# First chunk of a spectral mixer moved from tile to tile, its other chunks read in long runs, and GpSimd given more of the weight splitting

## The chip, the cores and the metric

The kernel runs on one core of one Trainium2 chip. The metric is the device time of one execution in microseconds: the median over the runs of the kernel before and after the change.

## The reference

One transformer-like block over x of 4096 rows and 640 columns, in float32: an adaptive layer norm, a Fourier mixer over the rows (AFNO), and a gated feed-forward part.

```python
mod = (silu(c) @ w_mod).reshape(1, 6, 1, 640)
sa, ca, ga, sb, cb, gb = (mod[:, i] for i in range(6))
h = layernorm(x) * (1 + ca) + sa
# AFNO: FFT over rows and columns axes (rfft2 with H = 1), 4 blocks of 160 channels,
# two complex layers w1, w2 with bias, ReLU between, soft threshold 0.01, inverse FFT
x = x + ga * irfft2(shrink(layer2(relu(layer1(rfft2(h))))))
h = layernorm(x) * (1 + cb) + sb
x = x + gb * ((silu(h @ w_gate) * (h @ w_up)) @ w_down)
```

## The kernel before

The Fourier transform of 4096 rows is made in two steps, 4096 = 128 x 32: row n is n1 * 32 + n2. **Stage A** works on 8 tiles `xa[t]` of 128 partitions (n1) and four values of n2, each a slice of 640 columns. For each tile DVE and GpSimd make the layer norm's statistics (`ln_stats`), ACT and DVE normalise (`ln_apply`), PE multiplies by the cosine and sine table `fa` (`dft_a`, line 407: four matmuls of 512 columns, one for each slice, and a fifth for the remaining 128 of all four) and ACT or DVE write the result back over the tile (`evac_a`, lines 414 to 418). The order of the columns of `fa` decides which frequency lands on which partition.

**Chunks.** The 128 partitions of a result hold eight chunks of 16 rows. **Stage B** wants one chunk at a time, with the 32 values of n2 on partitions, so the rows are turned through DRAM: `write_s1(t, f)` (line 338) writes the rows of tile t that belong to family f into the scratch tensor `s1[f]` (family 0: chunks 0 and 1, family 1: 2 and 3, family 2: 4 to 7), and `load_g(ch)` (line 307) reads a chunk back with four transfers into a tile `g` of 128 partitions and four slices of 640. Two such tiles exist (`gx`). A chunk can be read when all eight tiles of its family are written. Chunk 0 is read in two pieces: the rows of tiles 0 to 6 on GpSimd's queue, those of tile 7 on SyncE's queue.

**The loop.** Then a software pipeline of 32 steps p = 4 * ch + b runs over chunks and channel blocks: `stage_b` (line 542) finishes the transform into a PSUM bank, `evac_b` and `evac_r` (lines 549, 550, 572, 582) split it into a high and a low part for the rounded fp32r matmuls, `stage_l1` (603, 616) and `stage_l2` (649) are the two complex layers, `move_x` (665) turns the result `tt` by moves between tiles, `shrink` is the threshold, and `stage_i` the first half of the inverse transform, which writes to the scratch tensor `s2`. In the loop `mod_load` (478) brings pieces of `w_mod` into the buffer `wm`, and `mod_add` sums them on DVE. The feed-forward part comes after it.

**Weights.** `w1` and `w2` are split into high and low parts as well: `prep_weights` lists jobs for the tiles a, b and c (c holds the remainders), `weights_high` (280 on ACT, 278 on GpSimd) and `weights_low` (283 on DVE) do them. `w1` goes through ACT and DVE after stage A, the high parts of `w2` through GpSimd.

**Order.** All of this is one written order (`manual_schedule`): every engine and every queue executes its instructions in the order in which the code emits them, and SyncE's queue carries nearly all transfers. `moves(t)` emits what that queue does after tile t. The tiles `xa` and the pool `p2` (which holds `acc`, `cl`, `wx`, `bx`, `w2a` to `w2c`, `wm`, `tt`, `xx` and others) share the same memory, so an instruction that writes a `p2` tile waits until the rows of the `xa` tile beneath it are written out. PSUM has the tags b0 and b1 with one bank each and p1, p2, p3 with two each.

Of the kernel before, what the change touches and what calls it, by code (L numbers as in the profile page):

```python
# [9 lines left out]
OP = mybir.AluOpType  # L10
# [36 lines left out]
def constants():  # L47
# [9 lines left out]
    for ch in range(8):  # L57
        for p in range(2):
            for ri in range(2):
                for jj in range(4):  # L60
                    r = 4 * (2 * p + ri) + jj
                    m = 4 * (16 * (ch % 2) + r) + (0, 2, 1, 3)[ch // 2]
                    k = 2 * (4 * ORDER[ch] + jj) + p
                    th = tau * ((n1 * k) % 128) / 128
                    fa[:, m] = np.cos(th) if ri == 0 else -np.sin(th) if k else (-1.0) ** n1
# [106 lines left out]
def body(tc, x, w1, b1, w2, b2, wg, wu, wd, c, wm, k_fa, k_tb, k_tx, k_bm, k_bx, k_ga, k_ge, k_id, out, dbg=None):  # L172
# [8 lines left out]
    ov = out.rearrange("a b (n1 n2) d -> (a b n1) n2 d", n2=N2)  # L181
    s1 = [nc.dram_tensor(f"s1{f}", (n, N2, D), F32, kind="Internal").ap() for f, n in enumerate((32, 32, 64))]
    s2 = nc.dram_tensor("s2", (128, N2, D), F32, kind="Internal").ap()
# [16 lines left out]
    with ExitStack() as top:  # L200
# [33 lines left out]
        with ExitStack() as af:  # L234
# [49 lines left out]


            af.enter_context(tc.manual_schedule())
            nc.sync.dma_start(fa, k_fa)
# [10 lines left out]

            def load_g(ch, lo=0, hi=32, dma=None):
                if ch < 4:  # L300
                    src = s1[ch // 2].rearrange("(c q j) n d -> c q n j d", c=2, q=4)[ch % 2]
                else:
                    src = s1[2].rearrange("(c q j f) n d -> f c q n j d", c=2, q=4, f=2)[ch // 2 - 2, ch % 2]
                if lo == 0:
                    gs[ch] = fx.tile([P, 4, D], F32, tag="gx", bufs=2, name=f"g{ch}")
                for q in range(4):
                    (dma or nc.sync).dma_start(gs[ch][4 * lo + q:4 * hi:4], src[q, lo:hi])

# [15 lines left out]
            with tc.tile_pool(name="sp", bufs=1) as sp:  # L324
# [10 lines left out]


                def write_s1(t, f):
                    nc.sync.dma_start(s1[f][:, 4 * t:4 * t + 4, :], xas[t][(0, 2, 1)[f]:128:(4, 4, 2)[f]])

# [7 lines left out]

                def moves(t):
                    write_s1(t, 0)
                    if t == 0:  # L350
                        load_x(6)
                        nc.sync.dma_start(c5, c)
                    elif t == 1:
                        load_x(7)
                        raws[1] = load_weights(sp, w1, "1")
                    elif t == 2:
                        nc.sync.dma_start(wm1, wm[:, 1])
                    elif t == 3:
                        load_tb(0)
                        nc.sync.dma_start(b1m, b1[:, 0:8].rearrange("p (r b) -> p r b", r=2))  # L360
                        nc.sync.dma_start(b1r, b1[0:64, 8:12])
                        raws[2] = load_weights(rp, w2, "2")
                    elif t < 7:
                        if t == 6:
                            load_g(0, 0, 28, pool)
                        for f in (1, 2):
                            write_s1(t - 3, f)
                    else:
                        load_g(0, 28, 32)

# [29 lines left out]
                def dft_a(t):  # L400

                    xnr = xas[t].rearrange("p a (b e) -> p a b e", b=NB)
                    for i in range(5):
                        j = 5 * t + i
                        pa = (bank0(j // 4, [P, 512], f"pa{t}_{i}") if j % 4 == 0
# [4 lines left out]
                def evac_a(t):  # L410
                    xa = xas[t]
                    for i in range(5):
                        if t == 7 and i % 2:
# [9 lines left out]
                for t in range(8):  # L423
# [8 lines left out]
                    if t == 2:  # L432
                        act.activation(sc, c5, AF.Silu)
                    moves(t)

# [3 lines left out]
                for job in prep_weights(raws[1], w1a, w1b, w1c, True):  # L439
                    weights_high(*job)  # L440
                    weights_low(*job)

            hp = af.enter_context(tc.tile_pool(name="hp", bufs=1, reuse_waits="tile"))
            load_g(1)
            load_tb(1)
            b2t = hp.tile([P, 2, NB, BS], F32, name="b2t")
            nc.sync.dma_start(b2t, b2.rearrange("r b o -> (r b o)").partition_broadcast(P))
            for t in (0, 4, 5, 6, 7):
                write_s1(t, 1)
            load_g(2)  # L450
            load_tb(2)
            for t in (0, 4, 5, 6, 7):
                write_s1(t, 2)
            stx.close()

            nc.sync.dma_start(idn, k_id)
            nc.sync.dma_start(tx, k_tx)
            pool.dma_start(bm.rearrange("p a b c -> p (a b c)"), k_bm)
            p2 = af.enter_context(tc.tile_pool(name="p2", bufs=1, side="right", reuse_waits="tile"))

            acc = p2.tile([P, D], F32, name="acc")
            cl = p2.tile([P, D], F32, name="cl")
            wx = p2.tile([P, P], F32, name="wx")
            bx = p2.tile([P, 2, 128], F32, name="bx")
            w2a = p2.tile([P, NB, 640], F32R, name="w2a")
            w2b = p2.tile([P, NB, 640], F32R, name="w2b")
            w2c = p2.tile([P, NB, 640], F32R, name="w2c")
            prep2 = prep_weights(raws[2], w2a, w2b, w2c, False)
            for job in prep2:
# [6 lines left out]
            def mod_load(m, k):  # L476
                wmts[m, k] = p2.tile([P, D], F32, tag="wm", bufs=1, name=f"wm{m}_{k}")
                nc.sync.dma_start(wmts[m, k], wm[:, m, k, :])
# [57 lines left out]

            def stage_b(ch, t):
                g, tb = gs[ch], tbs[ch]
                pb = bank0(1 if t == 4 else 0, [P, 2, 256], f"pb{ch}_{t}")
                col = slice(128 * t, 128 * t + 128)  # L540
# [186 lines left out]


            for b in range(3):
                stage_b(0, b)  # L730
                if b == 0:
                    stage_b(0, 4)
                evac_b(0, b)
                evac_r(0, b)
# [33 lines left out]
            for p in range(LAST + 1):  # L768
# [28 lines left out]
                if p == 0:  # L797
                    for job in prep2[3:]:
                        weights_low(*job)
                if b == 3 and 2 < ch + 2 < NCH:  # L800
                    load_g(ch + 2)
# [9 lines left out]

            def load_first():
                x2 = fx.tile([P, 4, D], F32, tag="gx", bufs=2, name="x2_0")
                nc.sync.dma_start(x2, xv[:, 0:4, :])
                x2s[0] = x2
# [5 lines left out]
            for p in range(LAST + 1, NP):  # L821
# [4 lines left out]
                if p == LAST + 1:  # L826
                    on(shrink, p - 5)
                elif p == LAST + 2:
                    load_first()
                on(shrink_high, p - 5)  # L830
                on(stage_l2, p - 1)
                on(stage_i, p - 6)
                on(shrink_low, p - 5)
            on(shrink, LAST - 1)
            on(shrink_high, LAST - 1)
# [48 lines left out]
            def first_norm(i):  # L884
                mv, rs, nm = fst[i]
                xn = p2.tile([P, D], F32, tag="co" if i < 2 else "wm", bufs=2 if i < 2 else 1, name=f"xn0_{i}")
                act.activation(xn, x2[:, i, :], AF.Identity, bias=nm, scale=rs)
# [347 lines left out]
```

## Time and profile before

| | |
|---|---|
| runs of the kernel before | 1502.13, 1502.27, 1503.7 us; median 1502.27 us |
| profiled execution | 1502.37 us, its span 1500.6 us |
| PE busy | 1456.5 us, 97% of the span |
| DVE, ACT, POOL busy | 871.8, 587.7, 117.0 us |
| mean granted TensorE clock | 0.993 |

The span runs from the first instruction to the last; the profiled execution's time holds 1.8 us more. PE is TensorE's matmul row, DVE VectorE, ACT ScalarE, POOL GpSimd, SP SyncE; a "q" behind an engine's name means its queue of instructions that issue transfers. In the chain of waits a row gives the start, the length and what the end of the execution was waiting for then.

### The profile page before, as it was taken

The numbers are of one execution on the slowest core, as the hardware profiler recorded it, in microseconds if no ns is written. First come the engines' busy times: TensorE is split into PE (matmuls) and PEld (weight loads), VectorE is DVE, ScalarE is ACT, GpSimd is POOL, SyncE is SP. The second block draws the span as 40 slices with busy tenths as digits, with TensorE's granted clock in tenths as the row PEclk, the third lists the DMA queues.
The fourth block names the chain that finished last, engine by engine and source line by source line (L and its number), as shares of the span: only waits on it lengthen the run. The fifth ranks groups of instructions, "written<-read, shape, count | busy, mean of one in ns | idle before, by whom it ended". The sixth has DMA issues, their size and how long they took to land.

```text
span 1500.6 us, 20793 instructions
## 1 busy us (share of the span) xinstructions
PE 1456.5 (97%) x8114; PEld 1292.2 (86%) x8114; DVE 871.8 (58%) x1598; ACT 587.7 (39%) x1034; POOL 117.0 (8%) x215
## 2 busy tenths in 40 slices
PE   7599999989999999999999999999999999999998
PEld 2399999868989898989898989898889988898888
DVE  8478888877475437543844374447444744564433
ACT  7569989746232314231323132313231322223220
POOL 5400100030010001000100010001000100000000
PEclk9799999999999999999999999999999999999999
DMA  9946556647432423241324132513241324223210
GB/s 377 319 168 188 167 160 184 206 135 233 140 88 84 111 74 97 85 138 47 100 84 138 53 102 75 154 36 102 80 140 53 94 80 131 62 71 89 70 44 35
DMA packets 183057, 179.92 MB, mean 120 GB/s; under 512 B 19312, under 2 KB 153648, under 8 KB 180016
## 3 DMA queue, kind: packets, MB, share of 16 engines
q1 hardware_dynamic: 173728, 152.56, 34.0%
q0 software_dynamic: 3904, 14.91, 3.0%
q10 hardware_dynamic: 5328, 11.14, 2.0%
q8 instruction: 63, 1.03, 0.3%
q14 instruction: 34, 0.28, 0.1%
HBM read 137.95 MB, written 31.46 MB: 113 GB/s over the span
## 4 chain that ended last, share of the span: by engine, by line
PE 84%; DVE 5%; ACT 4%; DMA 4%; POOL 1%; SPq 1%; issue 1%; DVEq 0%; ACTq 0%; POOLq 0%
PE pd L1143 26%; PE pg L1050 8%; PE pg L1049 8%; PE pg L1051 8%; PE pu L1050 8%; PE pu L1049 8%; PE pu L1051 8%; PE pc L649 1%; PE pl L603 1%; PE pa L407 1%; DMA xx<-tt 1%; PE pb L542 1%; PE pt L1031 1%; DMA s<-xa 1%; DMA g<-s 1%
## 5 line engine op out<-in xcount | busy, mean ns | idle before, releaser
L1143 PE MATMUL pd<-wdh,ah 128*128 128x320 f32 x1664 | 384.4, 310 | 0.1
L1143 PEld LDWEIGHTS pd<-wdh,ah 128*128 128x128 f32 x1664 | 282.4, 188 | 1.0 <-DVE yo L1147 0.4
L1143 PE MATMUL pd<-wdl,ah 128*128 128x320 f32 x832 | 257.0, 309 | 0.0
L1044 DVE TENSOR_TENSOR wl<-wr,wh 128x640 fp32r<-128x640 f32 x216 | 177.5, 822 | 121.5 <-ACT wh L1043 121.5
L1050 PE MATMUL pg<-ht,wh 128*128 128x512 f32 x555 | 216.2, 389 | 0.0
L1049 PE MATMUL pg<-ht,wh 128*128 128x512 f32 x555 | 216.1, 389 | 0.0
L1051 PE MATMUL pg<-ht,wl 128*128 128x512 f32 x555 | 216.0, 389 | 0.0
L1049 PE MATMUL pu<-ht,wh 128*128 128x512 f32 x515 | 200.8, 390 | 0.0
L1050 PE MATMUL pu<-ht,wh 128*128 128x512 f32 x515 | 200.6, 390 | 0.0
L1051 PE MATMUL pu<-ht,wl 128*128 128x512 f32 x515 | 200.4, 389 | 0.0
L1107 ACT ACTIVATE sg<-pg 128x512 f32<-128x512 f32 x104 | 62.2, 598 | 336.2 <-PE pg L1051 335.3
L1120 ACT ACTIVATE ah<-sg 128x512 fp32r<-128x512 f32 x104 | 65.8, 632 | 295.4 <-DVE sg L1119 295.4
L1043 ACT ACTIVATE wh<-wr 128x640 fp32r<-128x640 f32 x216 | 157.1, 728 | 41.5 <-DVE x L1148 38.2
L1147 DVE TENSOR_TENSOR yo<-pd,gbb 128x320 f32<-128x320 f32 x128 | 62.7, 490 | 183.7 <-PE pd L1143 183.7
L1143 PEld LDWEIGHTS pd<-wdl,ah 128*128 128x128 f32 x832 | 156.3, 188 | 0.6
L1051 PEld LDWEIGHTS pg<-ht,wl 128*128 128x128 f32 x555 | 104.2, 188 | 21.8
L1119 DVE TENSOR_TENSOR sg<-pu,sg 128x512 f32<-128x512 f32 x104 | 71.7, 689 | 88.1 <-PE pu L1051 88.1
L1049 PEld LDWEIGHTS pg<-ht,wh 128*128 128x128 f32 x555 | 104.2, 188 | 21.0
L1050 PEld LDWEIGHTS pg<-ht,wh 128*128 128x128 f32 x555 | 104.2, 188 | 21.0
L1121 DVE TENSOR_TENSOR ah<-sg,ah 128x512 fp32r<-128x512 f32 x104 | 72.2, 694 | 72.7 <-ACT ah L1120 72.7
L1051 PEld LDWEIGHTS pu<-ht,wl 128*128 128x128 f32 x515 | 96.7, 188 | 20.3
L1049 PEld LDWEIGHTS pu<-ht,wh 128*128 128x128 f32 x515 | 96.7, 188 | 19.6
(209 smaller groups left out, 2001.6 us busy)
## 6 DMA issues: line engine op xcount, KB each, us to landing
wr<-in_B_w_gate_dram SPq DMA_DIRECT2D x104, 320.0 KB, 3.3
wr<-in_B_w_up_dram SPq DMA_DIRECT2D x104, 320.0 KB, 3.2
x<-in_A_x_dram SPq DMA_DIRECT2D x8, 1280.0 KB, 6.2
out_dram<-x ACTq DMA_DIRECT2D x31, 320.0 KB, 2.2
g<-s SPq DMA_DIRECT2D x28, 320.0 KB, 7.1
xx<-tt SPq DMA_DIRECT2D x56, 160.0 KB, 3.7
s<-co POOLq DMA_DIRECT2D x28, 320.0 KB, 3.4
cr<-s SPq DMA_DIRECT2D x28, 320.0 KB, 3.3
```

Source lines behind the costliest of these rows:

```text
L407: mm(pa, fa, xnr[:, i, :, 0:128] if i < 4 else xnr[:, :, :, 128:160], start=True, stop=True)
L1043: act.activation(wh, wr, AF.Copy)
L1044: dve.tensor_tensor(wl, wr, f32(wh), op=OP.subtract)
L1049: mm(pp, wh[:, k, :], ht[:, k, 0, :], start=(k == 0), stop=False)
L1050: mm(pp, wh[:, k, :], ht[:, k, 1, :], start=False, stop=False)
L1051: mm(pp, wl[:, k, :], ht[:, k, 0, :], start=False, stop=(k == 4))
L1107: act.activation(sg, pg, AF.Silu)
L1119: dve.tensor_tensor(sg, pu, sg, op=OP.mult)
L1120: act.activation(ah[:, 0, :], sg, AF.Copy)
L1121: dve.tensor_tensor(ah[:, 1, :], sg, f32(ah[:, 0, :]), op=OP.subtract)
L1143: mm(pd[:, :320], l, m, start=(i == 0), stop=(i == len(seq) - 1))
L1147: dve.tensor_tensor(yo, pd[:, :320], gbb[:, e], op=OP.mult)
```

## The change

1. `fa`'s columns are ordered anew: family 0 now holds 16 rows (chunk 1), on partitions 4 mod 8; family 1 lies on 2 mod 4 and family 2 on the odd partitions, as four rows of one chunk after four of the next. Chunk 0 lies on partitions 0 mod 8 and is in no family.
2. `place(t, i)`: for every tile and slice, 32 times in all, one transfer on SyncE's queue copies chunk 0's 16 rows of 640 columns straight from `xa[t]` to 4 partitions of `g0`.
3. `s1[f]` is laid out with n2 first; `write_s1` writes runs of one row and `load_g` reads a chunk as one transfer of 128 runs of 10 KB.
4. Early writes of families 1 and 2 are now those of tiles 0 and 1 (before: 1, 2 and 3); those of tile 2 follow behind `load_g(1)`, the others behind `b2t`. `w2a` to `w2c` come first in `p2` and lie on tiles 0, 1 and 2.
5. `dft_a` and `evac_a` take the fifth matmul first.
6. `stage_b` of the first four blocks (0, 4, 1, 2 of chunk 0) runs ahead of all their evictions, in banks b0, b1, p2 and p3.
7. GpSimd makes both parts of `w1c` (`weights_rest`), after tile 6.
8. `wm` has two buffers; `bm` is loaded at step 0 of the loop, the first rows of x from ACT's queue at the end of a step.

```diff
...
-                    r = 4 * (2 * p + ri) + jj
-                    m = 4 * (16 * (ch % 2) + r) + (0, 2, 1, 3)[ch // 2]
+                    q = 2 * p + ri
+                    m = (8 * (4 * q + jj) + 4 * ch if ch < 2 else 4 * (8 * q + 4 * (ch - 2) + jj) + 2 if ch < 4 else
+                         2 * (16 * q + 4 * (ch - 4) + jj) + 1)
...
-    s1 = [nc.dram_tensor(f"s1{f}", (n, N2, D), F32, kind="Internal").ap() for f, n in enumerate((32, 32, 64))]
+    s1 = [nc.dram_tensor(f"s1{f}", (N2, n, D), F32, kind="Internal").ap() for f, n in enumerate((16, 32, 64))]
     def layer_stats(pl, src, n, name):
...
+            def weights_rest(rr, wc):
+                pool.tensor_scalar(rr[:, 0], rr[:, 0], sgn[:, 0:1], None, op0=OP.mult)
+                for o in range(2):
+                    for oh, ol, n, src in [(128 * o, 256 + 128 * o, 128, 0), (512 + 32 * o, 576 + 32 * o, 32, 128)]:
+                        v = rr[:, o, :, src:src + n]
+                        pool.tensor_copy(wc[:, :, oh:oh + n], v)
+                        pool.tensor_tensor(wc[:, :, ol:ol + n], v, f32(wc[:, :, oh:oh + n]), op=OP.subtract)
...
-            def load_g(ch, lo=0, hi=32, dma=None):
-                if ch < 4:
-                    src = s1[ch // 2].rearrange("(c q j) n d -> c q n j d", c=2, q=4)[ch % 2]
-                else:
-                    src = s1[2].rearrange("(c q j f) n d -> f c q n j d", c=2, q=4, f=2)[ch // 2 - 2, ch % 2]
-                if lo == 0:
-                    gs[ch] = fx.tile([P, 4, D], F32, tag="gx", bufs=2, name=f"g{ch}")
-                for q in range(4):
-                    (dma or nc.sync).dma_start(gs[ch][4 * lo + q:4 * hi:4], src[q, lo:hi])
+            def load_g(ch):
+                f, n = (0, 1) if ch < 2 else (1, 2) if ch < 4 else (2, 4)
+                src = s1[f].rearrange("n (q e j) d -> e (n q) (j d)", e=n, q=4)[(ch - 1, ch - 2, ch - 4)[f]]
+                gs[ch] = fx.tile([P, 4, D], F32, tag="gx", bufs=2, name=f"g{ch}")
+                nc.sync.dma_start(gs[ch].rearrange("p j d -> p (j d)"), src)
             def remainders(src, rem):
...
+                gs[0] = fx.tile([P, 4, D], F32, tag="gx", bufs=2, name="g0")
+                def place(t, i):
+                    n = 4 * t + i
+                    nc.sync.dma_start(gs[0][4 * n:4 * n + 4], xas[t][0:128:8, i])
                 def write_s1(t, f):
-                    nc.sync.dma_start(s1[f][:, 4 * t:4 * t + 4, :], xas[t][(0, 2, 1)[f]:128:(4, 4, 2)[f]])
+                    nc.sync.dma_start(s1[f][4 * t:4 * t + 4].rearrange("n r d -> r n d"),
+                                      xas[t][(4, 2, 1)[f]:128:(8, 4, 2)[f]])
...
                 def moves(t):
+                    for i in range(4):
+                        place(t, i)
...
-                    elif t < 7:
-                        if t == 6:
-                            load_g(0, 0, 28, pool)
+                    elif t < 6:
-                            write_s1(t - 3, f)
-                    else:
-                        load_g(0, 28, 32)
+                            write_s1(t - 4, f)
                 def ln_stats(t):
...
                 def dft_a(t):
-                    for i in range(5):
-                        j = 5 * t + i
+                    for n, i in enumerate((4, 0, 1, 2, 3)):
+                        j = 5 * t + n
...
                 def evac_a(t):
-                    for i in range(5):
+                    for i in (4, 0, 1, 2, 3):
...
+                    if t == 6:
+                        weights_rest(raws[1][1], w1c)
-                    weights_high(*job)
-                    weights_low(*job)
+                    if job[0] is not w1c:
+                        weights_high(*job)
+                        weights_low(*job)
+            for f in (1, 2):
+                write_s1(2, f)
-            for t in (0, 4, 5, 6, 7):
-                write_s1(t, 1)
+            for t in (3, 4, 5, 6, 7):
+                for f in (1, 2):
+                    write_s1(t, f)
-            for t in (0, 4, 5, 6, 7):
-                write_s1(t, 2)
-            pool.dma_start(bm.rearrange("p a b c -> p (a b c)"), k_bm)
-            acc = p2.tile([P, D], F32, name="acc")
-            cl = p2.tile([P, D], F32, name="cl")
-            wx = p2.tile([P, P], F32, name="wx")
-            bx = p2.tile([P, 2, 128], F32, name="bx")
+            acc = p2.tile([P, D], F32, name="acc")
+            cl = p2.tile([P, D], F32, name="cl")
+            wx = p2.tile([P, 3 * P], F32, name="wx")[:, 0:P]
+            bx = p2.tile([P, 2, 128], F32, name="bx")
...
             def mod_load(m, k):
-                wmts[m, k] = p2.tile([P, D], F32, tag="wm", bufs=1, name=f"wm{m}_{k}")
+                wmts[m, k] = p2.tile([P, D], F32, tag="wm", bufs=2, name=f"wm{m}_{k}")
             def mod_add(m, k):
...
             def width(ch):
-            def stage_b(ch, t):
+            def stage_b(ch, t, tag=None):
-                pb = bank0(1 if t == 4 else 0, [P, 2, 256], f"pb{ch}_{t}")
+                pb = ps.tile([P, 2, 256], F32, tag=tag or ("b1" if t == 4 else "b0"),
+                             bufs=2 if tag and tag[0] == "p" else 1, name=f"pb{ch}_{t}")
...
+            for b, tag in ((0, "b0"), (4, "b1"), (1, "p2"), (2, "p3")):
+                stage_b(0, b, tag)
-                stage_b(0, b)
-                if b == 0:
-                    stage_b(0, 4)
...
+                    pool.dma_start(bm.rearrange("p a b c -> p (a b c)"), k_bm)
...
-            def load_first():
+            def load_first(q):
-                nc.sync.dma_start(x2, xv[:, 0:4, :])
+                q.dma_start(x2, xv[:, 0:4, :])
...
-                elif p == LAST + 2:
-                    load_first()
+                if p == LAST + 2:
+                    load_first(nc.scalar)
...
             def first_norm(i):
-                xn = p2.tile([P, D], F32, tag="co" if i < 2 else "wm", bufs=2 if i < 2 else 1, name=f"xn0_{i}")
+                xn = p2.tile([P, D], F32, tag="co" if i < 2 else "wm", bufs=2, name=f"xn0_{i}")
```

## The prediction

> **What bounds the kernel now.** I read first the page, whose profiled execution took 1502.37 us with a span of 1500.6 us (1.8 us lie around the span; the median of the runs is 1502.27 us, so both are the same time), then the busy time of each engine in stretches, because 97% busy PE over the whole span says nothing of the one place that this change touches.
>
> ```profile
> span 1500.6 us, 20793 instructions
> 45.00:50.00 5.00, 4.31 (x11) 1.65 (x10) 0.94 (x3) 4.15 (x9) 0.00 (x0) 1.00 0.99 415
> 50.00:55.00 5.00, 1.14 (x10) 1.06 (x10) 4.46 (x11) 5.00 (x14) 1.65 (x3) 0.64 0.71 283
> 55.00:60.00 5.00, 0.00 (x0) 0.00 (x0) 1.37 (x5) 0.27 (x2) 4.93 (x5) 0.50 0.96 234
> 60.00:65.00 5.00, 0.00 (x0) 0.00 (x0) 0.00 (x0) 0.00 (x0) 5.00 (x4) 0.50 1.16 254
> 65.00:70.00 5.00, 4.77 (x24) 4.45 (x24) 1.05 (x2) 1.76 (x4) 2.73 (x4) 0.66 1.05 422
> 70.00:75.00 5.00, 3.49 (x17) 3.49 (x18) 3.12 (x6) 3.10 (x6) 0.00 (x0) 0.69 0.41 172
> ```
>
> The columns after the stretch are PE, PEld, DVE, ACT and POOL busy, granted TensorE clock, DMA share, GB/s. From 51 to 65 us PE does nothing, its clock falls to 0.50 and is not whole again before 75 us. The chain of work that ended last says what that hole is:
>
> ```profile
> 40.33 8.87 PE pa L407 x20
> ...
> 50.82 4.74 DMA s<-xa
> ...
> 57.76 7.16 DMA g<-s
> 65.05 3.66 PE pb L542 x16
> ...
> 73.28 2.84 PE pl L603 x16
> ...
> 81.44 8.30 DMA s<-xa
> ...
> 90.42 2.62 PE pc L649 x16
> ...
> 96.42 2.37 PE pc L649 x16
> ```
>
> The last matmuls of the first transform end at 49.2 us; their rows go out to DRAM (4.74 us), come back as the first chunk g0 (the last read lands 7.16 us after 57.76), and only then does `stage_b` start. A second knot is at 81 to 90 us: the writes of the other rows (8.30 us) hold the memory in which `tt` lies, so the second `stage_l2` starts at 90.42. From there a step of the loop takes 96.42 - 90.42 = 6.0 us and PE is nearly full. So what the change is worth is how much earlier than 90.42 us PE reaches that same matmul group, plus what it does to the loop.
>
> **The change part by part.** *The places on SP.* The first chunk is no longer written and read; 32 transfers of 40 KB carry its rows from tile to tile. The sync queue issues them among everything else:
>
> ```profile
> 18.16 0.54 SPq L338 DMA_DIRECT2D s<-xa  x1
> 18.74 0.58 SPq L333 DMA_DIRECT2D xa<-in_A_x_dram  x1
> ...
> 55.58 5.43 SPq L307 DMA_DIRECT2D g<-s  x8
> 62.28 0.34 SPq L295 DMA_DIRECT2D tb<-in_k_tb_dram  x1
> ...
> SPq L295 <- DMA g<-s: 1.3, 1, 1.3
> ...
> xx<-tt SPq DMA_DIRECT2D x56, 160.0 KB, 3.7
> ```
>
> One issue takes 5.43/8 = 0.68 us in a burst, and the rows at 18 us give 0.58 without a wait between; I take 0.64. After eight issues the ninth (62.28) waits for the landing of an earlier one: about eight are in flight at most. From 18.2 us, where tile 0 is ready, to the last place there are 32 places, 7 writes of the second family's rows (`s1[0]`), 4 writes of tiles 0 and 1, and 11 loads: 54 issues, 54 x 0.64 = 34.6 us, so not before 18.2 + 34.6 = 52.8 us if the queue never waits. Before, it had 25 and waited for ACT. It will wait: the loads of `wm1`, `w1` and `w2` (1.6 and twice 1.28 MB, which take 10 us together at 415 GB/s) sit among the places, and eight in flight is less than two tiles' worth. I put 4 us on that, an estimate between 0 and the 10 us of those loads: last issue at 57 us. The tile-to-tile move that the trace has, `xx<-tt`, lands after 3.7 us at four times the size; with 3 us the chunk is complete at 60 us, against 64.9 us before. That is 5 us.
>
> What the move itself costs on the DMA engines the trace does not show for this shape (16 rows of 2560 B onto 4 neighbouring partitions). The lower end is 40 KB at the full 415 GB/s, 0.1 us; the upper end is one of sixteen engines, 415/16 = 26 GB/s, 1.6 us. No row is nearer to the one end than to the other, so I take the middle by ratio, 0.4 us (four of the sixteen engines): 32 x 0.4 = 12.6 us beside 34 us of other traffic, which hides because the halved first write gives back 8 x 160 KB (3 us) and one tile's other writes, 960 KB (2.3 us), move behind the places. Both ends stay in the rivals.
> The Trainium skill, page "DMA: Bandwidth & Descriptors", section "Why a DMA increments its semaphore by 16 and not by 1", says that a transfer runs on the largest number of engines, up to 16, that divides the slowest dimension of both sides; for 16 rows onto 4 that makes four engines, on which the sum would come out as it stands.
>
> *The order 4, 0, 1, 2, 3.* The fifth matmul of a tile needs all four slices normalised, so PE can start a tile later, by at most one ACT slice of about 1 us in the last tile; the last eviction (50.8 us) moves by some tenths. Nothing, against the queue's 57 us that covers it.
>
> *Four banks.* Before, block 1 waited for block 0's evictions and block 2 for block 1's; from 65.05 to 73.28 us, 8.2 us passed for four blocks. Now all four run one after another: 16 matmuls took 3.66 us at clock 0.50, 32 take 7.3 us at that clock, and ACT and DVE evict beneath them. One us gained, `stage_l1` at about 67.5 us instead of 73.
>
> *GpSimd and the second weights.* This part sets how far the 5 us reach.
>
> ```profile
> 53.34 2.64 POOL L307 DMA_DIRECT2D g<-s  x4 [12.26 <-DMA s<-xa]
> ...
> 56.63 1.84 POOL L278 TENSOR_SCALAR w2a<-rm 128x640 fp32r<-128x640 f32 x1
> ...
> 83.19 0.82 DVE L283 SCALAR_TENSOR_TENSOR w2c<-rr,w2c 128x640 fp32r<-128x640 f32 x1
> 83.54 0.69 PE L649 MATMUL pc<-w2a,h 128*128 128x320 f32 x3
> ```
>
> POOL stands idle for the 12.26 us before 53.34. `weights_rest` fills that: one scaling of 1.84 us and, twice, a copy and a subtraction of 512 and of 128 columns, at the 1.84/640 us per column of L278 1.5 + 1.5 + 0.4 + 0.4 = 3.7 us: 9.2 us in all, double for the subtractions at worst, 13 us. It ends at 50 to 54 us, before `stage_l1` wants w1c: free, hidden by the wait for g0; were g0 there at 53 us already, it could cost up to 1 us. Then the six L278 scalings of `w2`, 1.84 us each. The new order of tiles puts w2c on the memory of tile 2, whose writes are issued only behind `load_g(1)`, which waits for the last `s1[0]` write to land (about 60.5 us). The read of g1, 1.28 MB, is 3.1 us at 415 GB/s and about 2 us of delay: 65.5 us; tile 2's 960 KB are 2.3 us more plus the delay: 68.5 us. Only then w2c's first scaling (70.3), three more (75.9), DVE's L283 (76.7): `stage_l2` of block 0 starts at 76.7 us against 83.54, and DVE, in order, holds the evictions of the loop behind these waits, so PE idles some us here. The second `stage_l2` follows one step of 6.0 us later, 82.7 us, against 90.42: **7.7 us gained**. The old knot at 81 us does not return: tiles 3 and 4, under `tt`, are written by 65.5 + 3.8 MB/415 GB/s = 75 us.
>
> *In the loop.* One issue per chunk instead of four saves SP 3 x 0.64 us six times, the runs of 10 KB shorten the read, and `wm` has two buffers:
>
> ```profile
> SPq L478 <- DMA wm<-in_w_mod_dram: 9.0, 3, 3.3
> ...
> 140.00:160.00 20.00, 18.60 (x147) 18.34 (x146) 16.82 (x35) 17.87 (x37) 1.08 (x2) 1.00 0.59 185
> ```
>
> PE is short 1.4 us in this stretch of 20, and a part of it comes from DVE behind a late `wm`. I take 1 us for the loop, between 0 and 3. The first rows of x on ACT's queue, and `bm` later on POOL's: one issue each, behind which ACT's next eviction and POOL's next write wait well under 1 us, both late against nothing; zero.
>
> Sum: 7.7 + 1.0 = 8.7 us; 1502.4 - 8.7 = 1493.7, say 1493.5 us.
>
> **The rivals.** *One sixteenth of the rate (slower).* If all 16 rows of a place must enter through one narrow way, it takes 1.6 us instead of 0.4, four take 6.3 us where a tile has 8.87/2 = 4.4 us, and 32 take 50 us. They stand in the same rings as x, the weights and the writes (34 us of full DMA from 18 to 52 us), so on the engines they use these add: 18 + 34 + 50 - 5 given back = 97 us for the chunk instead of 64.9. The rest of the start shortens by 3 us as above (7.7 gained where the chunk itself comes 5 earlier): 29 us lost, about 1531 us. It decides from about 0.65 us for a place: 32 x 0.25 = 8 us over the forecast's value, and the gain is gone; at 0.8 us, two sharing a way, it is 1507 us. For it speaks that the destination is 4 neighbouring partitions; against it, that no row shows such a narrow place, and reads and writes of strided rows here run at 415.
> The Trainium skill, page "SBUF — State Buffer", section "Door 1: The DMA port swizzle", says that four neighbouring partitions share one of 16 ports of about 27 GB/s; the trace's 26 GB/s for each of 16 engines agrees with the figure, and no transfer of before shows the four-partition case. By that rule the time would be the 1531 us of this rival.
>
> *The places are spread over all engines.* Then 0.1 us each, the queue waits for nothing but its issues: last place at 53 us, the chunk at 56, every later step 4 us earlier: 1489.5 us. Nothing in the trace forbids it; the queue's eight in flight speak against.
>
> *The gain is lost at w2c.* If the transfers of tile 2 land behind more of the queue (b2t and the tiles after it share the engines), POOL's last scaling slips from 75.9 to 82 us and `stage_l2` starts where it did, 83 us; only the 81 us knot is saved, in part: 1500 us.
>
> **How the numbers follow.** A difference of 0.2% is 3 us, about what a measurement of this kernel can tell. The forecast (1490 to 1499) gets 0.46, the spread places 0.16, both faster: 0.62. The loss at w2c within 3 us: 0.05. Places at 0.75 to 0.95 us, 1505.5 to 1512 us: 0.15; the full narrow way, 1512 to 1535: 0.18; slower 0.33. I give the range without the last one: from 1486 (spread places and 3 us in the loop) to 1512. The faster cases' own range is 1486 to 1499.
>
> **What would show it.** Right: in the chain, g0 comes from `xa` directly with the last landing near 60 us, PE's hole ends there, `pc` of block 0 starts near 77 us, and POOL works from 41 us on. SP's waits should be for landings of its own transfers. Wrong: `xa<-in_A_x_dram` landing later than before and PE short already between 30 and 50 us (narrow places); PE idle between 67 and 83 us with POOL waiting for `s<-xa` (w2c); or no shift of the 90.42 us group although g0 comes early.

## The result, and the profile after

The kernel after takes 1508.16 us (median of 6 runs, 1506.44 to 1509.01), the kernel before on the same chip 1502.2 us: ratio 1.0038, 95% interval 1.0025 to 1.0051. It is slower by 6 us where 8.7 us of gain were forecast. The profiled execution took 1509.01 us.

The span (the profile page after), and the chain of waits of the kernel after:

```profile
span 1507.2 us, 20802 instructions
```
```profile
27.99 9.58 DMA xa<-in_A_x_dram
37.59 3.25 DVE st_a L192 x8
...
48.25 4.57 PE pa L419 x10
...
65.88 0.54 SPq L348
66.48 2.82 DMA s<-xa
69.43 5.28 PE pb L558 x24
...
80.00 2.67 POOL w2c L279
...
91.13 2.54 PE pc L665 x16
...
97.04 2.35 PE pc L665 x16
```

The last place is issued at 65.88 us, not at 57, and `stage_b` starts at 69.43 where it started at 65.05 before. (The landing of a place can't be matched here; the chain names the write issued right behind the last one.) The second group of `stage_l2`, on which the forecast was built, stands at 97.04 instead of 90.42: 6.6 us late, and the span is 6.6 us longer (both profiles need 1410.2 us from that group to the end). So all of the loss arises before 97 us, and the loop gives nothing back. Tile 7 of x lands at 37.59 us and stage A ends late, and the chain passes through both, because it puts a wait of SP at 57 us down to ACT. SP's own row below shows that it had no time to spare there, and e1 that an earlier x gains nothing. The SyncE queue is (view of its instructions in order of time; groups with start, time of issuing and count):

```profile
20.08 2.72 SPq L348 DMA_DIRECT2D g<-xa  x4
...
47.93 0.56 SPq L250 DMA_DIRECT2D rm<-in_A_w_dram  x1
48.53 0.43 SPq L251 DMA_DIRECT2D rr<-in_A_w_dram  x1
49.07 2.58 SPq L348 DMA_DIRECT2D g<-xa  x4
51.71 2.07 SPq L351 DMA_DIRECT2D s<-xa  x3
55.00 3.00 SPq L348 DMA_DIRECT2D g<-xa  x4
58.05 1.91 SPq L351 DMA_DIRECT2D s<-xa  x3
60.07 3.15 SPq L348 DMA_DIRECT2D g<-xa  x4
63.28 0.58 SPq L351 DMA_DIRECT2D s<-xa  x1
63.95 2.47 SPq L348 DMA_DIRECT2D g<-xa  x4
66.48 0.57 SPq L351 DMA_DIRECT2D s<-xa  x1
```

From 48 us to 67 SP issues nearly without a break: the rows of tile 4, written back by ACT at 41 us, are placed only at 49 us. Before that it waited for landings (view of waits on SP's queue, total, times, longest):

```profile
SPq L348 <- DMA rr<-in_A_w_dram: 2.9, 2, 1.8
...
SPq L377 <- DMA wm<-in_w_mod_dram: 1.9, 1, 1.9
SPq L373 <- DMA xa<-in_A_x_dram: 1.8, 1, 1.8
SPq L250 <- DMA xa<-in_A_x_dram: 1.4, 1, 1.4
SPq L348 <- DMA rm<-in_A_w_dram: 1.2, 1, 1.2
```

And the stretch from 20 to 50 us, which I took for cover, shows in its last column (GB/s) what became of the transfers; first the kernel before, then after:

```profile
20.00:50.00 30.00, 27.37 (x62) 10.98 (x62) 24.87 (x72) 28.72 (x49) 10.03 (x20) 1.00 1.01 419
```
```profile
20.00:50.00 30.00, 27.45 (x62) 11.18 (x61) 22.88 (x69) 29.29 (x51) 16.04 (x26) 1.00 0.85 283
```

(419 - 283) GB/s x 30 us = 4.1 MB less were moved, 9.8 us of DMA at 415 GB/s. PE and ACT did the same work in it, DVE 2 us less.

### The profile page after: what moved, and what is told of

Read it like the earlier page. It is cut to its first block, busy times and chain, and to the rows that moved or that the text cites. A ratio compares the mean times of both kernels' runs of the same rounds, so it can differ in the third digit from the quotient of the medians.

```text
span 1507.2 us, 20802 instructions
## 1 busy us (share of the span) xinstructions
PE 1457.2 (97%) x8114; PEld 1294.6 (86%) x8114; DVE 872.8 (58%) x1594; ACT 585.8 (39%) x1030; POOL 125.6 (8%) x220
## 4 chain that ended last, share of the span: by engine, by line
PE 84%; ACT 5%; DVE 4%; DMA 3%; SPq 2%; issue 1%; POOL 1%; ACTq 0%; DVEq 0%
PE pd L1159 26%; PE pg L1066 8%; PE pg L1065 8%; PE pg L1067 8%; PE pu L1066 8%; PE pu L1065 8%; PE pu L1067 8%; PE pc L665 2%; DMA xa<-in_A_x_dram 2%; PE pl L619 2%; PE pb L558 1%; DMA xx<-tt 1%; PE pt L1047 1%; SPq L681 1%; DVE st_a L192 1%
## 5 line engine op out<-in xcount | busy, mean ns | idle before, releaser
L1163 DVE TENSOR_TENSOR yo<-pd,gbb 128x320 f32<-128x320 f32 x128 | 62.7, 490 | 184.0 <-PE pd L1159 184.0
```

The source lines that it names most:

```text
L1163: dve.tensor_tensor(yo, pd[:, :320], gbb[:, e], op=OP.mult)
```

## The experiments

Eighteen kernels were run. The table has, for each, the DMA rate from 20 to 50 us and the start of the first `stage_b` (both from its one profile), the median, and the ratio to the kernel before on the same chip.

| kernel | GB/s | stage_b | us | ratio (95%) |
|---|---|---|---|---|
| before | 419 | 65.1 | 1502.2 | |
| after | 283 | 69.4 | 1508.2 | 1.0038 (1.0025 to 1.0051) |
| e1 x first | 276 | 69.9 | 1508.3 | 1.0050 (1.0032 to 1.0068) |
| e2 four ports | 291 | 67.5 | 1506.2 | 1.0037 (1.0024 to 1.0050) |
| e3 half the bytes | 300 | 65.5 | 1504.6 | 1.0025 (1.0015 to 1.0034) |
| e4 chunk 0 via DRAM | 369 | 63.8 | 1500.0 | 0.9997 (0.9986 to 1.0008) |
| e5 after, order 0 to 4 | 281 | 69.4 | 1507.3 | 1.0038 (1.0025 to 1.0052) |
| e6 via DRAM, order 0 to 4 | 411 | 59.6 | 1497.0 | 0.9967 (0.9950 to 0.9984) |
| e7 e6, tile 2 early | 415 | 60.5 | 1498.2 | 0.9976 (0.9966 to 0.9985) |
| e8 before, order 4 first | 374 | 67.6 | 1502.5 | 1.0008 (0.9995 to 1.0020) |
| e9 e6 and 32 tiny places | 330 | 70.7 | 1508.0 | 1.0039 (1.0025 to 1.0054) |
| e10 after, 16 partitions | 296 | 64.8 | 1505.4 | 1.0021 (1.0011 to 1.0032) |
| e11 e10, order 0 to 4 | 297 | 65.6 | 1508.7 | 1.0045 (1.0030 to 1.0060) |
| e12 e6, two banks | 410 | 59.6 | 1495.5 | 0.9960 (0.9946 to 0.9975) |
| e13 after, loads on GpSimd | 299 | 71.4 | 1509.9 | 1.0065 (1.0050 to 1.0080) |
| e14 e13, order 0 to 4 | 304 | 70.5 | 1509.7 | 1.0058 (1.0041 to 1.0075) |
| e15 e12, loads on GpSimd | 414 | 58.8 | 1496.3 | 0.9969 (0.9959 to 0.9979) |
| e16 before, one long read | 407 | 62.4 | 1496.9 | 0.9967 (0.9957 to 0.9978) |
| e17 e5, 16 places on GpSimd | 301 | 62.7 | 1508.2 | 1.0042 (1.0025 to 1.0059) |
| e18 e12 and 16 tiny places | 317 | 66.2 | 1503.2 | 1.0011 (1.0000 to 1.0021) |

No kernel that has places, tiny ones included, is above 330 GB/s, and none of them is faster than before; those without are at 369 to 419.

**First set: which part of the change.** My theory after the result was that places on four DMA engines hold up the loads behind them (A); rivals were SP's issuing (B), the port of four neighbouring partitions (C) and the w2c chain (D).

e1: `load_x` for all eight tiles ahead of the places.

> The changed kernel with the loads of x tiles 6 and 7 issued before the first place, instead of behind the places of tiles 0 and 1; nothing else. Theory A (the places use few of the DMA engines, and every load queued behind them on those engines waits): tile 7 of x lands near 32 us instead of 37.6, stage A's last matmul ends near 50 us instead of 52.8, the execution is 2 to 4 us shorter than the changed kernel's 1508.2, about 1505. Theory B (the sync queue's 55 issues and its eight transfers in flight set the last place): the number of issues is the same, last place still issued at 65 to 66 us, no change within 1.5 us. Theory C (four neighbouring partitions are one narrow way into the memory): as A.

x arrived on time (tile 7's statistics at 34.9 us, as before) and nothing was gained: lateness of x is a symptom. Stage A's last matmul still ended at 53.5 us, not near 50; the reason is the order of its matmuls, below.

e2:
```diff
-                    nc.sync.dma_start(gs[0][4 * n:4 * n + 4], xas[t][0:128:8, i])
+                    nc.sync.dma_start(gs[0][16 * t + i:16 * t + 16:4], xas[t][0:128:8, i])
```

> The changed kernel with the four rows of each place put on partitions four apart (16t+i, +4, +8, +12) instead of on four neighbours; the table of chunk 0 is permuted to match. Theory C: each place is up to four times as quick, the load of x tile 7 lands 4 us earlier, the chunk is complete by 62 us, 5 us or more shorter than the changed kernel (1503 or less). Theories A and B: same number of engines and issues, no change within 1.5 us of 1508.

The ratio is that of the kernel after. By medians e2 is 2 us below e1, which ran beside it, and its first `stage_b` comes 1.9 us earlier than in the kernel after; theory C asked for 5 us or more. So the four neighbouring partitions are at most a small part of the cause. The Trainium skill, page "SBUF — State Buffer", section "Door 1: The DMA port swizzle", gives four neighbours one port; by it the forecast's rival had 1531 us. No run here shows such a price.

e3:
```diff
-                    nc.sync.dma_start(gs[0][4 * n:4 * n + 4], xas[t][0:128:8, i])
+                    nc.sync.dma_start(gs[0][4 * n:4 * n + 4, :, 0:320], xas[t][0:128:8, i, 0:320])
```

> The changed kernel with each place carrying 320 of the 640 columns (the other half of chunk 0 is left at zero by one early write of VectorE, so half of chunk 0 is left out of the result): the same 32 issues, half the bytes. Theory A: half the time on the few engines, x tile 7 lands about 3 us earlier, last place 3 to 5 us earlier, 3 to 5 us shorter than 1508.2. Theory B: no change within 1.5 us. Theory C: as A.

About 3.6 us come back by the medians (1508.2 to 1504.6; the intervals of the ratios overlap), which I read as support for A; SP's last write of family 0 goes out at 63.40 us instead of 66.48. The tiny places below show that the bytes are the smaller part.

e4: family 0 holds chunks 0 and 1 again, no places, `load_g(0)` as one read of 10 KB runs behind tile 7.

> The changed kernel with chunk 0 back in the first family: written to DRAM with chunk 1 and read back as one transfer of 10 KB runs; no places; the four banks, the GpSimd weights, the order of writes, the two wm buffers stay. Theories A, B and C alike put the loss on the places: chunk 0 complete near 61 us, second group of stage_l2 near 88 us instead of 97, the execution 7 to 10 us shorter than the changed kernel, 1498 to 1501, at or a little below the kernel before. Rival D (the other parts lose: tile 2's writes behind the read of g1, GpSimd late with w2c): 1505 or more even without places.

The places cost 8 us by the medians (1508.2 to 1500.0; also against e1, which ran beside e4) and 6 by the ratios to the kernel before. The first `stage_b` starts at 63.8 us, where a complete chunk near 61 was expected. The other parts came out near zero together, so I took out the order as well.

**Second set: the order 4, 0, 1, 2, 3 and the w2c chain.** The edit of e5 and e6, whose reverse on the kernel before is e8:
```diff
-                    for n, i in enumerate((4, 0, 1, 2, 3)):
+                    for n, i in enumerate(range(5)):
...
-                    for i in (4, 0, 1, 2, 3):
+                    for i in range(5):
```

> The changed kernel with stage A's matmuls and evictions back in the order 0, 1, 2, 3, 4; the places and everything else stay. Theory O (the new order costs stage A some 3.5 to 4 us: the first matmul of a tile waits for all four normalised slices, and ACT's first eviction writes columns that all five matmuls read): stage A's last matmul ends near 50.5 us instead of 52.8. If the new order alone set the end, the execution falls by 3 to 4 us to about 1504.5. Theory A (the sync queue and the few engines of the places are behind anyway): the last place is still issued after 64 us and the execution stays within 1.5 us of 1508.

> Chunk 0 through DRAM and the order 0, 1, 2, 3, 4: of the change there stay the long runs, the four banks, the GpSimd weights, the order of writes and the two wm buffers. Theory O: without the places stage A's end decides, 49.2 instead of 53.65 us, chunk 0 near 59.5 us, 3 to 4 us shorter than the kernel with chunk 0 through DRAM alone (1500): about 1496.5, 4 us below the kernel before. Rival (the order costs nothing, stage A's end is late for another reason such as GpSimd's weights): 1500 as without it.

> The kernel before with one part of the change alone: stage A's matmuls and evictions in the order 4, 0, 1, 2, 3. Theory O: stage A's last matmul ends at 52.5 to 53.5 us instead of 49.2, chunk 0 and everything behind it 3.5 to 4.3 us later, about 1505 where the kernel before gives 1501. Rival (the order costs nothing): 1501.

With the places in, the order costs nothing measurable; without them it costs 3 us by the medians, 4.5 by the ratios (e4 to e6); on the kernel before at most 3, likeliest 1 us, where about 4 were expected. PE's matmuls of stage A, first in e4, then in e6 (idle time and its releaser in brackets):

```profile
29.03 4.56 PE L416 MATMUL pa<-xa,fa 128*128 128x512 f32 x10 [0.48 <-ACT xa L398]
34.62 4.56 PE L416 MATMUL pa<-xa,fa 128*128 128x512 f32 x10 [1.03 <-ACT xa L398]
...
49.08 4.56 PE L416 MATMUL pa<-xa,fa 128*128 128x512 f32 x10 [0.77 <-ACT xa L398]
```
```profile
31.74 17.74 PE L416 MATMUL pa<-xa,fa 128*128 128x512 f32 x40 [1.81 <-ACT xa L398]
```

With the fifth matmul first PE waits anew for the last normalised slice; the waits add up and stage A ends at 53.7 us instead of 49.5.

e7: the writes of tile 2 go out in stage A (`elif t < 7` in `moves`).

> As the kernel with chunk 0 through DRAM and the old order, and tile 2's writes of families 1 and 2 issued in stage A after tile 6 instead of behind the read of g1. Theory D (GpSimd's w2c, which lies on tile 2, sets the second layer's start): GpSimd's third w2 scaling starts near 60 us instead of 68 to 72, the first group of stage_l2 5 us earlier, 3 to 5 us shorter than with tile 2 late: about 1492. If D is wrong (chunk 0 and the loop's start decide): no change or 1 us longer, since two more transfers stand before the read of chunk 0.

The last w2 scaling starts at 59.9 us instead of 72.5, and the time stays that of e6: by then the row of evictions on ACT and DVE and of w2 splits on DVE, 64 to 75.6 us in the chain of e7, ends last before the restart of PE. D is no cause; one wait stood behind another.

**Third set: engines or queue.** e9 adds to e6 the 32 places with 16 columns instead of 640; e10 keeps 40 KB and spreads each place over 16 partitions; e11 is e10 in the order 0 to 4; e12 undoes the four banks in e6.
```diff
+                    nc.sync.dma_start(gs[0][4 * n:4 * n + 4, :, 0:16], xas[t][0:128:8, i, 0:16])
```
```diff
-                    nc.sync.dma_start(gs[0][4 * n:4 * n + 4], xas[t][0:128:8, i])
+                    nc.sync.dma_start(gs[0][16 * t:16 * t + 16, i], xas[t][0:128:8, i])
```

> The kernel of e6 (chunk 0 through DRAM, order 0 to 4; 1497.0 us), to which the 32 places are added as tiny transfers: same count, same partitions, same queue, but 16 columns of each row instead of 640, so 1 KB instead of 40 KB; the read of chunk 0 overwrites what they bring. If the bytes on few DMA engines are what the places cost, the 32 issues of 0.55 us hide in SP's waits for ACT and it stays within 2 us of e6: 1497 to 1499, the first stage_b within 1 us of 59.6. If it is SP, with 32 more issues and its waits for landings in order, most of the loss shows: 1503 to 1507, the first stage_b at 65 us or later.

> The kernel after, with one thing changed: each place puts its 16 rows of 640 columns onto 16 partitions, one row on each, instead of four rows on each of 4 partitions (chunk 0's rows then lie permuted in its tile, so the numbers of the output differ). Issues, bytes, packets and order stay. If the 4 engines are the cause, the transfers now spread over all 16, loads of x, wm and w1 come in on time, and the last place is issued near 59 us instead of 65.9: 1499 to 1502 us, that of chunk 0 through DRAM (1500.0) or a little below. If it is the count of issues and SP's waits for landings whatever the engines, it stays at 1505 to 1508.

> e10 and the matmuls and evictions of stage A in the order 0 to 4 as before. With the few engines as the cause, this is the forecast's case of spread places: 1494 to 1498 us, first stage_b near 57 us, no later than e6's 59.6. With SP's count of issues as the cause: 1504 to 1507, as the order alone gave (1507.3).

> The kernel of e6 (1497.0 us) with the first blocks of stage_b in two banks as before. The forecast's term for four banks is 1 us: 1498 us. If DVE's row of evictions and w2 splits ends last before stage_l2 (69 to 77 us in e6 and e7) rather than PE, two banks cost nothing: 1496.5 to 1497.3. If PE's restart at the clock 0.50 is what ends last, up to 3 us: 1500.

Theory A is at most the smaller part. 32 transfers of 1 KB cost e6 11 us, more than the whole change. The last write of family 0 on SP (its row in the chain), first in e6, then in e9, then in e5 with 40 KB for each place:

```profile
51.12 2.56 DMA s<-xa
```
```profile
62.19 2.58 DMA s<-xa
```
```profile
66.40 2.91 DMA s<-xa
```

Of the 15.3 us by which 40 KB places delay it, 11.1 are there with 1 KB each; the places' bytes add 4.2, although e9's writes of family 0 carry these rows too, 320 KB each instead of 160. (e9 still reads chunk 0 through DRAM behind that write, so its total does not show the gain of the 4.2 us.) Spread over 16 partitions the places keep the loss (e11, against e5) or most of it (e10, 2.8 us better by medians); in both the second `stage_l2` group comes at 94.2 us, about 3 us earlier than in the kernel after and in e5. What counts most is that 32 more transfers stand in SP's queue. e12 is no slower than e6, so the four banks bring nothing measurable, though `stage_l1` starts at 64.7 us with them and at 67.5 without.

What a place holds while it waits is in the DMA issues of e11, where landings are known (count, size, median us from issue to landing):

```profile
g<-xa SPq DMA_DIRECT2D x32, 40.0 KB, 4.7
```

40 KB at 415 GB/s are 0.1 us. In e11 the places take from 9.8 us, among the loads, down to 2.3 us at the end; so some 2.4 of the 4.7 us are the wait behind the transfers issued before, an estimate. In e10, e11 and e12 all landings on SP are known, and counted from them never more than eight of its transfers are open at once. The trace's records show where the eight comes from: SP's transfers use eight completion semaphores in turn, and until 55 us every issue from the ninth on waits for its own semaphore, that is, for the landing of the transfer eight before it. So the eight slots are in this program's waits; no run shows whether the queue has a limit of its own. In the kernel after, SP's pauses of over 0.15 us between the first and the last place sum to 11.9 us, and 11.4 of them end within 0.12 us after such a landing. In the kernel before none does between 18 and 51 us; there SP pauses 18.6 us, nearly all of it for ACT.

32 places of 4.7 us occupy 150 us of the 8 x 47 us of slots between 17.4 and 64.7 us, an estimate of 40%. A slot that held 640 KB or 1.28 MB holds 40 KB, and the rate falls: from 20 to 50 us 5.6 transfers with 3.4 MB are open on average in e12 and 6.9 with 2.4 MB in e11, counted from the same landings. Two sections of the Trainium skill's page "DMA: Bandwidth & Descriptors" fit this: "Queues, rings and completion order" says that an engine takes the descriptors of a ring in their order, and "Rules for kernel authors" advises to join many small transfers, those under 64 KB being mostly overhead. The 4.7 us agree with both; the limit of eight is not in them.

**Fourth set: which part of SP's time, and where the gain is.** In e13 to e15 eight loads (`c5`, `w1`, `w2`, `wm1`, `b1m`, `b1r`) go to GpSimd's queue (`nc.sync` becomes `pool` on those lines). e16 is the kernel before with only the new layout of `s1`, `load_g` as one transfer, and chunk 0 read behind tile 7.

> The kernel after (1508.2 us) with eight loads (c5, w1 and w2 with two transfers each, wm1, b1m, b1r) issued on GpSimd's queue instead of SP's; the 32 places, their bytes, their four engines and their queue stay. If SP's queue is the cause: 46 issues instead of 54 up to the last place, 8 x 0.58 = 4.6 us less, and of its 15.2 us of gaps those before and behind these loads (1.45, 1.84, 1.28, 1.84, 1.92 = 8.3 us) go: last place at 53 to 58 us instead of 65.9, first stage_b at 57 to 62 instead of 69.4, 1497 to 1502 us. If the four engines are the cause, the bytes collide as before: last place after 62 us, 1505 to 1509.

> e13 with the order 0 to 4 in stage A. SP's queue as the cause: with the order's cost gone too, last place at 52 to 57 us and 1494 to 1499 us, the forecast's 1493.5 at the lower end. Four engines as the cause: 1504 to 1508, as e5 (1507.3).

> e12 (chunk 0 through DRAM, order 0 to 4, two banks; 1495.5 us) with the same eight loads on GpSimd's queue. There SP waits 23 us for ACT and has no backlog, so taking eight issues off it should do nothing: 1494.5 to 1497. If it gained more than 2 us, the loads' queue would matter by itself, and e13 and e14 could not be read as tests of the places' queue.

> The kernel before with the new layout of the scratch tensors alone: chunks read in one transfer of 10 KB runs on SP, chunk 0 through DRAM in one read behind tile 7's write; order, banks, w2's place, weights_rest and wm as before. If the one read is where the versions through DRAM gain, the first stage_b starts near 60 us instead of 65.0 (e6 59.6), and the old knot of tt on tiles 3 and 4 at 81 to 90 us gives some of it back: 1498 to 1500. If their gain comes from w2's new place and the other parts, this one stays at 1501 to 1503.

e13 and e14 met neither expectation and tell nothing of the queue: free of SP's order, the moved loads ran ahead of x, tile 7's statistics started at 48.3 and 45.2 us, and stage A itself ended at 64.8 and 58.4. e15 is the control and stays with e12. e16 is the find: the new layout with its long reads alone makes 4.7 us, as much as the versions through DRAM have within their intervals. In the kernel before chunk 0 took eight transfers, four on GpSimd's queue and four of 40 KB on SP, where they share a row of eight issues of 0.68 us with chunk 1's; the last landed at 64.9 us. In e16 it is one, issued at 56.86 us and landed at 62.4. GpSimd, which no longer waits to issue a read, starts `w2` at 50.0 us instead of 56.6; how much of the 4.7 us is due to that no run shows.

e17: places of tiles 4 to 7 on GpSimd's queue, `w1c` on ACT and DVE again. e18: e12 and tiny places for tiles 0 to 3 alone.
```diff
-                    nc.sync.dma_start(gs[0][4 * n:4 * n + 4], xas[t][0:128:8, i])
+                    (nc.sync if t < 4 else pool).dma_start(gs[0][4 * n:4 * n + 4], xas[t][0:128:8, i])
```

> e5 (the kernel after with the order 0 to 4; 1507.3 us) with the 16 places of tiles 4 to 7 issued on GpSimd's queue, and w1c made by ACT and DVE as before, so that GpSimd is free for them. Bytes and engines of the places stay. If SP's row of issues is the cause: in e5 SP works without a break from 48 to 67 us; 16 x 0.6 = 9.6 us of it go, the last write of family 0 goes out at 52 to 56 us, the first stage_b runs at 57 to 60 instead of 69.4, and it is 1494 to 1499 us. If the places' bytes on four engines are the cause, the chunk is complete after 63 us and it is 1502 to 1507.

> e12 (chunk 0 through DRAM, order 0 to 4, two banks; 1495.5 us) with tiny places (1 KB each, overwritten later) for tiles 0 to 3 alone, 16 more issues on SP, all before about 42 us. In e12 SP waits 20 us and more for ACT and the last write of family 0 goes out at 50.7 us, in e9 with 32 tiny places at 62.2. If only the late row of issues costs, SP catches up by tile 7: at most 1 us, 1495 to 1497. If early issues push x, w1 and wm back and the delay stays, half of e9's loss shows: the last write at 54 to 57 us, 1500 to 1503.

e18 shows the loss without the bytes and without the late row. Its 16 issues take SP 16 x 0.58 = 9.3 us, and from the first to the last of them SP pauses 9.5 us for slots, against 1.3 us in all of e12 until 50.7 us; together they use up the 18 us and more that SP waits for ACT in e12. SP's queue, first in e12, then in e18:

```profile
29.57 0.59 SPq L370 DMA_DIRECT2D wm<-in_w_mod_dram  x1
...
36.87 0.61 SPq L250 DMA_DIRECT2D rm<-in_A_w_dram  x1
...
53.89 0.81 SPq L313 DMA_DIRECT2D g<-s  x2
```
```profile
34.98 0.33 SPq L379 DMA_DIRECT2D wm<-in_w_mod_dram  x1
...
44.20 0.58 SPq L250 DMA_DIRECT2D rm<-in_A_w_dram  x1
...
60.55 0.81 SPq L314 DMA_DIRECT2D g<-s  x2
```

`wm1` goes out 5.4 us and `w2` 7.3 us later, and the read of chunk 0 6.7 us later, although the last write is issued at 53.81 us against 50.68: it takes 6.60 us to land (chain of e18) where e12's takes 3.1, and the late loads and writes stand ahead of it.

```profile
53.81 6.60 DMA s<-xa
...
60.55 5.53 DMA g<-s
```

16 KB in 16 transfers cost 7.7 us of time (1503.2 against 1495.5, from two sets). e17 fulfilled half: SP's last write goes out at 55.8 us as expected, `stage_b` starts at 62.7 instead of 69.4 (57 to 60 expected), and the stretch to 50 us is as empty as with all places on SP (301 GB/s); but the time did not follow. At 90 us e17 stands where the kernel before does and at the first feed-forward matmul 4.3 us behind it. Part of that goes with TensorE's granted clock, 0.90 in this stretch of e17 against 1.00 before (a tenth of 10 us, an estimate of 1 us); the rest I can't name:

```profile
300.00:310.00 10.00, 7.60 (x46) 7.12 (x45) 8.34 (x17) 6.26 (x15) 1.08 (x2) 0.90 0.57 197
```

**What stays open.** How much of the loss is SP's 0.58 us for each issue and how much the eight slots. From the first to the last place SP issues for 31.1 us and waits for slots for 11.4 us; with 1 KB each (e9) it is 31.3 and 10.5 us. But no run has the issues without the slots, so what each would cost alone isn't shown. How the bytes make their 4 us (by few engines, by their time in a slot or otherwise). The later loss of e17, and of e11: it has the second `stage_l2` where e10 has it and a span 5.3 us longer.

**Versions that beat both kernels** are e6, e7, e12, e15 and e16, their intervals overlapping. The smallest edit of them is e16: 1496.9 us, 0.9967 (0.9957 to 0.9978) of the kernel before.

## Why the prediction was wrong, point by point

- *The places on SP, last issue at 57 us.* The count was right: 54 issues between the first and the last place, 0.58 us each, 31.1 us. The term that failed is the wait, "I put 4 us on that". The gaps between issues sum to 15.2 us; 3.3 of them (54 x 0.06) are in my 0.64 us, so it was 12 us, beyond even the upper end of 10 us that I gave that term; 11.4 of them are waits for one of the eight slots. The first place came at 20.08 instead of 18.2 us, which is the order. Together 65.9. I had read "about eight are in flight at most" from the kernel before and priced only the waits for the big loads; that the small ones themselves fill the eight slots I did not price.
- *12.6 us of places hide beside 34 us of other traffic.* Wrong in kind. The price in bytes is not measured by itself; nearly all of the bytes together moved SP's last write by 4.2 us (e9 against e5). What was at stake was the cover: the other traffic's rate, which I took as given at 415 GB/s, fell to 283 with the places in.
- *The order costs nothing against the queue's 57 us.* True in the kernel after (e5) and for the reason given. The size under it was wrong: stage A's last eviction moved from 50.8 to 54.8 us by the order alone (e8), not by tenths, and uncovered it costs 3 us or more (e4 to e6).
- *Four banks, 1 us.* `stage_l1` follows `stage_b` after 5.9 us instead of 7.9 (my 8.2 came from a row of the chain that begins after the group's first matmuls), so the step was there; e12 shows no time for it.
- *w2c.* From the chunk to the first `stage_l2` I had 16.7 us; it is 91.13 - 69.43 = 21.7. Tile 2's writes held w2c until 80 us, not 68.5; they were issued at 70.2 and 71.8 us, behind a chunk that is itself late. This was the third rival's mechanism, and e7 shows that its removal brings nothing, DVE being next.
- *Rival of one sixteenth.* It ended on the right side for the wrong reason: neither ports (e2) nor engines (e10, e11) make most of the loss. That 1508.2 us lies in the band that I gave to places of 0.75 to 0.95 us is luck: what a place costs is a turn in a queue.
- *The loop, 1 us.* 6.6 us late at 97 us and 6.6 us in the span: nothing.
- *Sum.* Forecast and profile differ by 8.7 + 6.6 = 15.3 us: 9.4 at the chunk (69.4 against 60), 5.0 from there to `stage_l2`, 1 in the loop. The 5 us that the chunk was to bring can be had from the other half of the change: e6 starts `stage_b` at 59.6 us with no place at all.

## What to carry to other kernels

Before adding transfers to a queue that feeds a full DMA stretch, count its open transfers and the completion semaphores that the program gives it, not only its issues and bytes: a small transfer behind large ones can hold a slot for as long as they take (up to 9.8 us for 40 KB here). A GB/s column that is flat and full is a resource in use, not cover for more work. Where a chunk is read in many strided pieces, change the layout so that one transfer reads it, and try that alone first.

## What was not expected of the hardware

Transfers of 1 KB delay SP's queue nearly as much as those of 40 KB: 11.1 against 15.3 us at its last write. The DMA's busy share does not tell its rate: from 30 to 40 us it is 1.02 at 340 GB/s in e10,

```profile
30.00:40.00 10.00, 8.70 (x21) 3.45 (x20) 9.12 (x29) 9.97 (x17) 4.99 (x10) 1.00 1.02 340
```

and 1.00 at 415 GB/s in the kernel before:

```profile
30.00:40.00 10.00, 8.56 (x20) 3.67 (x20) 9.48 (x30) 9.99 (x18) 5.24 (x10) 1.00 1.00 415
```
